# Coarse product, additions and tokens one step later in a software-pipelined attention, MoE and FFN kernel

## The chip, the cores and the metric

One core of a Trainium2 chip runs one program. The metric is device time in microseconds (us) of one execution, the median of several runs. Engines: PE (matrix products and transposes), DVE (vector), ACT (scalar), POOL (GpSimd), and the SP queue, which issues the DMA transfers. Each engine works through its own list in program order and waits by semaphores for the others.

## The reference, cut to what matters

```python
# attention: B=4, H=8, S=576, D=64; every part below feeds the next
q_d, k_d, v_d = (mean over groups of 4 rows of q, k, v)           # 144 coarse rows
out_up = repeat(softmax(q_d @ k_d.T / 8) @ v_d, 4)                # coarse attention
mask = |i - j| < 4
out_local = softmax(where(mask, q @ k.T / 8, -1e9)) @ v           # band of 7 keys
x = (out_up + out_local) as [2304, 512]                           # tokens
# soft MoE: 8 experts of 4 slots each
logits = x @ phi;  d = softmax over tokens;  slots = d.T @ x
slot_out[e] = relu(slots[e] @ w1[e]) @ w2[e]
x = softmax over slots(logits) @ slot_out
# FFN
out = relu(x @ w_in) ** 2 @ w_out
```

## The kernel before, in words

The attention is cut into 16 **units** (one batch and two heads each; four units make a batch). A unit passes through some twenty small steps, each a function that the program calls by a letter. The string `ORDER` lists these letters once; the loop `for s in range(3, NU)` calls the whole string in every **step** s, and gives each letter the unit that it works on: a letter of unit s-3 belongs to work begun three steps earlier. So one step touches units s to s-3, and the order in which each engine meets its instructions is the order of the letters. Nothing reorders them afterwards. `START` and `DRAIN` are lists written by hand for the filling and the emptying of the pipeline.

The letters, with the unit that they take in step s:

- `Q` loads q and k (unit s+2), `L` loads v (s-1), `l` loads a few weight pieces for the later stages.
- `T` (s): twelve PE transposes of q and k (tiles `tr`, L389), read out by ACT (`q`, L395) and by ACT and DVE (`kz`, L397). `d` (s): POOL sums groups of four rows into `qkd`.
- `S` (s-1): the local scores on PE (tile `s`), then on DVE the maximum `mx` (L427) and the subtraction into `elp` (L428). `E`: ACT's exponential of `elp` (L433).
- `s` (s-1): the coarse scores on PE (`sd`); `m`: their maximum on DVE (L447); `e`: three exponentials on ACT into `pd` (L454).
- `n`, `N` (s-1): sums and reciprocal on DVE, the scalings on POOL (`pl`, `pd`).
- `p` (s-2): transposes of the local probabilities (`ptp`), read out by ACT into `pt` (L482). `q` (s-2): transposes of the coarse probabilities (`pdp`), read out by ACT into `pdt` (L494).
- `V` (s-3): the local product on PE into two PSUM banks `av`, which carry sums of v along (L506). `x`: these sums are copied to `vt` (L516). `X`: two PE transposes of `vt` (`vdp`, L526), copied by DVE to `vd` (L527). `D`: the coarse product on PE from `vd` and `pdt` into the second bank `av` (L536), read out by ACT into `xd` (L541). `A`: DVE adds `av` and `xd` into the tokens `xt` (L549).
- `t` (s-3): the logits of the tokens (`lgt`, L567) and five transposes of `xt` (`xp`, `xrp`), read out by ACT (`xk`, `xr`). For the last unit of a batch `t` also runs the batch's softmax over tokens (`stage_g1`: a chain DVE, ACT, DVE), and one step later `g` and `G` transpose its result and form the batch's sums on PE (`stage_g2`, `stage_g3`, tile `sip`).
- `c`: DVE turns pieces of w_in from 64-bit to 32-bit words ("narrowing", L226 to L232): a turn of five phases, two instructions each. `CONV` says how many phases step s takes.

All transposes share one PSUM tag of three buffers (`bt`), so a transpose waits until the third one before it has been read out. `av` has two buffers, which are the two banks of one unit: `V` of the next unit waits until `A` has read them. `vt`, `vd`, `xd`, `xt`, `pt`, `elp`, `pl`, `pd`, `pdt` have one buffer each.

After the attention the experts and the FFN follow (from about 222 us to the end), which the change does not touch.

## Time and profile before

| | |
|---|---|
| time, median of 3 runs | 505.5 us (503.65 to 506.02) |
| the profiled execution's own time | 500.57 us |
| its span, first to last instruction | 498.9 us |
| busy share of the span | PE 89%, DVE 57%, ACT 54%, POOL 19% |
| mean granted clock of PE | 0.928 of full speed |
| weights, q, k and v read | 65.07 MB, 140 GB/s over the span |

The span holds stages with different limits: the attention to about 222 us, the experts to about 262 us, then the FFN. [...] A busy PE in the profile includes the modelled end of each product, so busy time is no measure of work when the clock is low.

### The profile page before, as it was taken

Reading aid. Unit: us, or ns where it says so; the run is one execution under the profiler, and the core shown is the slowest. Engines: PE = TensorE matmul, PEld = TensorE weight load, DVE = VectorE, ACT = ScalarE, POOL = GpSimd, SP = SyncE. Lnnn points to the kernel's source line nnn. Section 1 sums busy time; section 2 is a strip of 40 time slices with the busy share of each in tenths; the row PEclk is TensorE's granted clock in tenths of the full one; section 3 lists DMA queues with packets and bytes.
Section 4 is the critical chain, followed back from the end, with each engine's and each line's share of the span. In section 5 each row is a group of like instructions: output and inputs, shape, how many; then the busy total and the mean of one; then the engine's idle time right before and its main releaser. Section 6 shows DMA issues by size and latency. Waiting matters only on the chain.

```text
span 498.9 us, 10561 instructions
## 1 busy us (share of the span) xinstructions
PE 446.2 (89%) x4130; PEld 339.0 (68%) x4130; DVE 286.8 (57%) x624; ACT 267.6 (54%) x681; POOL 95.2 (19%) x169
## 2 busy tenths in 40 slices
PE   6687879788988778789998899999999999999996
PEld 5465656566666555554546678788888888888884
DVE  5655465645565566432408999994654645546452
ACT  5576555556454453322248889887544444444441
POOL 8255444444443333200200000000000000000000
PEclk9799878977787778899999999999999999999999
DMA  8966853854555534499999900000300100100101
GB/s 198 309 202 195 246 154 103 245 159 136 164 165 155 154 112 152 148 328 359 397 400 409 367 2 0 2 0 1 127 0 1 64 1 0 64 1 27 38 0 64
DMA packets 48875, 70.47 MB, mean 141 GB/s; under 512 B 23866, under 2 KB 30266, under 8 KB 48826
## 3 DMA queue, kind: packets, MB, share of 16 engines
q1 hardware_dynamic: 48682, 69.67, 42.7%
q8 instruction: 32, 0.52, 0.4%
q14 instruction: 17, 0.14, 0.1%
q10 hardware_dynamic: 144, 0.13, 0.1%
HBM read 65.07 MB, written 4.72 MB: 140 GB/s over the span
## 4 chain that ended last, share of the span: by engine, by line
PE 71%; DVE 15%; ACT 10%; issue 2%; DMA 1%; DVEq 0%; ACTq 0%
PE po L1029 36%; PE sd L443 4%; PE hp L837 3%; PE s L419 3%; PE ptp L481 3%; PE so L861 3%; PE up L969 3%; PE av L536 3%; ACT pd L454 3%; DVE kz L397 2%; PE pdp L493 2%; PE tr L389 2%; DVE win L231 2%; PE av L506 2%; ACT q L395 2%
## 5 line engine op out<-in xcount | busy, mean ns | idle before, releaser
L1029 PE MATMUL po<-wparts,ghi 128*128 128x512 f32 x576 | 149.1, 392 | 2.3 <-DVE wparts L927 2.3
L1029 PEld LDWEIGHTS po<-wparts,ghi 128*128 128x128 f32 x576 | 106.7, 188 | 23.8 <-DVE wparts L927 3.7
L974 ACT ACTIVATE r<-up 128x384 f32<-128x384 f32 x96 | 46.9, 489 | 72.8 <-PE up L969 68.6
L1029 PE MATMUL po<-wparts,glo 128*128 128x512 f32 x288 | 81.6, 391 | 0.5 <-DVE glo L982 0.5
L978 DVE TENSOR_TENSOR r<-r 128x384 f32<-128x384 f32 x64 | 35.6, 556 | 58.6 <-ACT ghi L977 58.6
L1029 PEld LDWEIGHTS po<-wparts,glo 128*128 128x128 f32 x288 | 53.9, 188 | 12.3 <-DVE glo L982 1.2
L982 DVE TENSOR_TENSOR glo<-r,ghi 128x384 fp32r<-128x384 f32 x94 | 52.3, 557 | 13.6 <-ACT ghi L981 7.5
L977 ACT ACTIVATE ghi<-r 128x384 fp32r<-128x384 f32 x66 | 34.7, 526 | 2.1
L969 PE MATMUL up<-cst,ast 128*128 128x384 f32 x96 | 33.0, 345 | 0.7 <-DVE ast L960 0.4
L395 ACT ACTIVATE q<-tr 64x288 f32<-64x288 f32 x64 | 27.2, 426 | 10.2 <-PE tr L389 9.4
L467 POOL TENSOR_TENSOR pl<-elp,sm 64x350 f32<-64x350 f32 x30 | 24.9, 831 | 26.3 <-DVE sm L465 11.5
L427 DVE TENSOR_REDUCE mx<-s 128x10 f32<-128x350 f32 x16 | 8.4, 522 | 33.3 <-PE s L419 33.2
L482 ACT COPY pt<-ptp 128x464 f32<-128x464 f32 (+1 forms) x32 | 11.3, 407 | 29.7 <-PE ptp L481 29.7
L407 POOL TENSOR_TENSOR qkd<-s 128x144 f32<-128x144 f32 x30 | 12.8, 425 | 74.0 <-PE sd L443 59.2
L506 PEld LDWEIGHTS av<-pt,vw 64*64 64x64 f32 x640 | 22.6, 139 | 3.5 <-issue 2.3
L506 PE MATMUL av<-pt,vw 64*64 64x73 f32 (+1 forms) x640 | 25.0, 232 | 0.0
L536 PE MATMUL av<-pdt,vd 72*64 72x144 f32 x128 | 15.0, 369 | 9.8 <-DVE vd L527 9.8
L389 PE MATMUL tr<-ident,k 96*128 96x96 f32 x96 | 15.2, 271 | 9.4 <-ACT q L395 9.0
L443 PE MATMUL sd<-qkd 64*64 64x144 f32 x192 | 22.6, 391 | 0.0
L397 DVE COPY kz<-tr 64x288 f32<-64x288 f32 x32 | 14.6, 458 | 12.4 <-PE tr L389 12.0
L541 ACT ACTIVATE xd<-av 128x288 f32<-128x288 f32 x16 | 6.6, 410 | 28.2 <-PE av L536 28.2
L969 PEld LDWEIGHTS up<-cst,ast 128*128 128x128 f32 x96 | 17.9, 188 | 5.2 <-DVE ast L960 0.7
(193 smaller groups left out, 729.7 us busy)
## 6 DMA issues: line engine op xcount, KB each, us to landing
w<-in_moe_w_dram SPq DMA_DIRECT2D x64, 512.0 KB, 6.4
win<-in_moe_w_in_dram SPq DMA_DIRECT2D x16, 512.0 KB, 7.7
wout<-in_moe_w_out_dram SPq DMA_DIRECT2D x16, 512.0 KB, 10.2
vw<-in_v_dram SPq DMA_DIRECT2D x30, 160.0 KB, 4.3
q<-in_q_dram SPq DMA_DIRECT2D x16, 288.0 KB, 3.2
k<-in_k_dram SPq DMA_DIRECT2D x16, 288.0 KB, 4.0
out_dram<-o SPq DMA_DIRECT2D x17, 256.0 KB, 2.3
vw<-in_v_dram SPq DMA_DIRECT2D x2, 144.0 KB, 5.6
```

Source lines behind the costliest of these rows:

```text
L389: nc.tensor.transpose(t[:, :, i], st[nm][:, h, 128 * i:128 * i + 128], ident[0:96, 0:96])
L395: nc.scalar.mul(out=o, in_=i_, mul=1.0 / 128.0)
L443: nc.tensor.matmul(sd[rr, t], qkd[rr, 0, 48 * t:48 * t + 64], qkd[rr, 1, 0:144], start=True, stop=True)
L467: (nc.vector if u in NDVE else nc.gpsimd).tensor_tensor(out=pl[r, :, c0:c0 + W], in0=el[r], in1=sm[r, 0:NB].unsqueeze(2).to_broadcast([64, ...
L506: nc.tensor.matmul(av[a][rr, VC * i:VC * i + n], vw[rr, 2 * i + a], pt[rr, i, a, 0:n], start=True, stop=True, tile_position=(64 * h, 64 * ...
L536: nc.tensor.matmul(dn[rr], st["vd"][:, a, rr], st["pdt"][:, a, :, h], start=(a == 0), stop=(a == 1), skip_group_check=True,)
L969: nc.tensor.matmul(t, ast[:, 128 * f:128 * f + 128], cst[:, c * n:c * n + n], start=True, stop=True)
L974: nc.scalar.activation(out=r, in_=t, func=AF.Relu)
L977: nc.scalar.activation(out=ghi, in_=r, func=AF.Square)
L978: nc.vector.tensor_tensor(out=g, in0=r, in1=r, op=ALU.mult)
L982: nc.vector.tensor_tensor(out=glo, in0=g, in1=ghi, op=ALU.subtract)
L1029: nc.tensor.matmul(po[c][i], a[:, 128 * i:128 * i + 128], w[f], start=(f == 0 and w is whi and a is ghi), stop=(f == NF - 1 and a is glo), ...
```

## The change

`T` now only transposes q; the keys get a letter of their own, `K`, which stands behind the scores `S` and `s`. `D` and `A`, and with them the tokens `t` (and `g`, `G` after them), move to the next step: they take unit s-4 and not s-3. `D` and `A` open the step. `pd` and `pdt` get two buffers, since the coarse probabilities now live one step longer. Both copies into `vt` go to DVE (the first was ACT's). `START` and `DRAIN` are written to match.

```diff
-ORDER = "VxTXQLgDSApsEdmqenGtNlc"
+ORDER = "DTAgSEsmKQdVxLepGtnXNqlc"
-START = "T0 Q2 d0 f10 T1 Q3 S0 s0 E0 d1 m0 T2 Q4 e0 f2 n0 l3 N0 S1 p0 s1 E1 q0 d2 m1 e1 n1 N1 l3"
+START = "T0 K0 Q2 d0 f10 T1 K1 Q3 S0 s0 E0 d1 m0 T2 K2 Q4 e0 f2 n0 l3 N0 S1 p0 s1 E1 q0 d2 m1 e1 n1 N1 l3"
-DRAIN = "V13 x13 L15 l3 p14 X13 D13 A13 S15 E15 s15 a m15 q14 e15 n15 N15 l c1 V14 x14 t13 X14 D14 A14 c1 p15 q15 V15 x15 X15 f1 D15 l c1 t14 A15 f6 t15 l"
+DRAIN = "D12 S15 A12 V13 x13 L15 l3 g2 E15 s15 a G2 t12 m15 p14 X13 q14 e15 n15 N15 l D13 c1 A13 V14 x14 t13 p15 X14 q15 D14 A14 V15 x15 c1 t14 X15 f1 D15 l c1 A15 f6 t15 l"
...
-        def transposes(u):
+        def transposes(u, js=(0,)):
             st = U[u]
-            for j, nm in enumerate("qk"):
+            for j in js:
+                nm = "qk"[j]
...
-            pd = ap.tile([128, 3, 144], F32, tag="pd", name=f"pd{u}")
+            pd = ap.tile([128, 3, 144], F32, tag="pd", bufs=2, name=f"pd{u}")
...
-            pdt = ap.tile([72, 2, 3, 2, 48], F32, tag="pdt", name=f"pdt{u}")
+            pdt = ap.tile([72, 2, 3, 2, 48], F32, tag="pdt", bufs=2, name=f"pdt{u}")
...
-            for a, c0, n, copy in ((0, 0, NC0, nc.scalar.copy), (1, NC0, NC1, nc.vector.tensor_copy)):
-                copy(
+            for a, c0, n in ((0, 0, NC0), (1, NC0, NC1)):
+                nc.vector.tensor_copy(
...
-                **dict.fromkeys("SEsmenN", u1), **dict.fromkeys("pq", u2), **dict.fromkeys("VxXDAt", u3),
+                **dict.fromkeys("SEsmenN", u1), **dict.fromkeys("pq", u2), **dict.fromkeys("VxX", u3), **dict.fromkeys("DAt", u4),
...
-                    if last(u4):
-                        (stage_g2 if x == "g" else stage_g3)(u4 // NP)
+                    if last(u5):
+                        (stage_g2 if x == "g" else stage_g3)(u5 // NP)
...
-                if x == "T" and s >= NU - 2:
+                if x == "K" and s >= NU - 2:
                     free.extend((ring, f"{y}{s % 2}") for y in "qk")
```

What this does on PE, at step 5 (the number behind a tile's name is its unit; for `ptp` and the others the first number). Before, from V(2) to p(3):

```order
L506 MATMUL av2_0_754<-pt_146,vw0_130 64x73 x10
L506 MATMUL av2_1_755<-pt_146,vw0_130 64x72 x10
L389 MATMUL tr5_00_779<-ident_67,q5_479 128x96 x3
L389 MATMUL tr5_01_785<-ident_67,q5_479 128x96 x3
L389 MATMUL tr5_10_791<-ident_67,k5_481 128x96 x3
L389 MATMUL tr5_11_797<-ident_67,k5_481 128x96 x3
L526 MATMUL vdp2_804<-ident_67,vt2_776 72x128 x2
L536 MATMUL av2_1_755<-pdt2_710,vd2_803 64x144 x4
L413 LDWEIGHTS identb_72
L413 MATMUL s4_819<-maskb_120,identb_72 128x350
L419 MATMUL s4_819<-kz0_139,q0_136 29x70 x20
L481 MATMUL ptp3_0_848<-ident_67,pl_165 128x128 x4
```

Now the step opens with D(1) and the transposes of q(5), and V(2) comes behind the scores and the keys:

```order
L390 MATMUL tr5_00_734<-ident_67,q5_484 128x96 x3
L390 MATMUL tr5_01_740<-ident_67,q5_484 128x96 x3
L414 LDWEIGHTS identb_72
L414 MATMUL s4_749<-maskb_120,identb_72 128x350
L420 MATMUL s4_749<-kz0_139,q0_136 29x70 x20
L444 MATMUL sd4_776<-qkd_161 64x144 x6
L390 MATMUL tr5_10_784<-ident_67,k5_486 128x96 x3
L390 MATMUL tr5_11_790<-ident_67,k5_486 128x96 x3
L507 MATMUL av2_0_807<-pt_146,vw0_130 64x73 x10
L507 MATMUL av2_1_808<-pt_146,vw0_130 64x72 x10
L482 MATMUL ptp3_0_838<-ident_67,pl_165 128x128 x4
L482 MATMUL ptp3_4_844<-ident_67,pl_165 128x128
```

In the first list X (`vdp`) follows the transposes and D follows X at once. In the second, D(1) opens the step (the row `av1_1<-pdt1,vd1`), S follows the transposes of q, and V(2) stands behind K. The end of the same step, from the transposes of the tokens on, holds the X(2) and D(2) of that V:

```order
L577 MATMUL xp1_855<-ident_67,xt1_746 128x128 x4
L580 MATMUL xrp1_861<-ident_67,xt1_746 64x128
L527 MATMUL vdp2_870<-ident_67,vt2_829 72x128 x2
L494 MATMUL pdp3_0_876<-ident_67,pd3_669 72x112 x3
L494 MATMUL pdp3_1_881<-ident_67,pd3_669 72x112 x3
L537 MATMUL av2_1_808<-pdt2_712,vd2_869 64x144 x4
```

X(2) is now followed by six transposes of `pd` before D(2) wants its result.

On DVE, around the narrowing of step 4 (`win`), the rows before:

```order
L465 RECIPROCAL sm3_679<-sm3_679 128x13
L229 TENSOR_SCALAR win0_0_588<-win0_0_588 128x512 x2
L516 COPY vt2_776<-av2_1_755 128x5x14
L397 COPY kz1_144<-tr5_11_797 64x288 x2
L527 COPY vd2_803<-vdp2_804 72x256
L427 TENSOR_REDUCE mx4_841<-s4_819 128x10
L428 TENSOR_TENSOR elp_163<-s4_819,mx4_841 128x10x35
L549 TENSOR_TENSOR xt2_845<-av2_0_754,xd_159 128x5x58
L549 TENSOR_TENSOR xt2_845<-av2_1_755,xd_159 128x5x58
```

and the rows now:

```order
L465 TENSOR_SCALAR sm3_607<-sd3_611 128x3
L466 RECIPROCAL sm3_607<-sm3_607 128x13
L528 COPY vd1_706<-vdp1_707 72x256
L229 TENSOR_SCALAR win0_0_561<-win0_0_561 128x512 x2
L550 TENSOR_TENSOR xt1_746<-av1_0_642,xd_159 128x5x58
L550 TENSOR_TENSOR xt1_746<-av1_1_643,xd_159 128x5x58
L428 TENSOR_REDUCE mx4_771<-s4_749 128x10
L429 TENSOR_TENSOR elp_163<-s4_749,mx4_771 128x10x35
L448 TENSOR_REDUCE mx4_771<-sd4_776 128x3
```

Before, the additions (`xt`) stood behind `mx` and `elp` of the scores, and the copies of the next unit right behind the narrowing. Now the additions of unit 1 stand between the narrowing and `mx4`, and both copies to `vt` are DVE's. The SP queue issues the same transfers in the same order as before, and the number of PE instructions is the same.

## Rows read from the trace of the kernel before

**Rows 1.** Stretches: length; busy of PE, PEld, DVE, ACT, POOL (instructions); PEclk; DMA share; GB/s.

```profile
40.13:49.96 9.83, 8.34 (x150) 6.47 (x148) 5.81 (x14) 6.76 (x21) 5.32 (x8) 1.00 0.71 203
...
60.30:74.66 14.36, 11.54 (x151) 8.75 (x150) 7.75 (x19) 7.74 (x26) 6.02 (x8) 0.74 0.60 161
...
30.32:181.57 151.25, 125.13 (x1792) 93.45 (x1791) 86.80 (x193) 84.64 (x269) 67.45 (x97) 0.83 0.59 171
...
181.57:222.08 40.51, 33.90 (x431) 24.00 (x429) 20.42 (x52) 14.08 (x48) 8.33 (x12) 0.87 0.53 184
```

**Rows 2.** Timeline of one step: start us, duration us, engine, line, instruction [idle before it].

```profile
41.83 0.70 ACT L482 COPY pt<-ptp 128x464 f32<-128x464 f32 x2 [1.17 <-PE ptp L481]
...
41.90 0.52 DVE L428 TENSOR_TENSOR elp<-s,mx 128x350 f32<-128x350 f32 x1
...
42.33 0.82 DVE L549 TENSOR_TENSOR xt<-av,xd 128x290 f32<-128x290 f32 x2
...
42.45 0.49 ACT L433 ACTIVATE elp<-elp 128x350 f32<-128x350 f32 x1
...
42.71 0.80 PE L493 MATMUL pdp<-ident,pd 112*72 112x112 f32 x6
...
43.85 0.39 ACT L454 ACTIVATE pd<-sd,mx 128x144 f32<-128x144 f32 x1
...
44.54 1.48 PE L506 MATMUL av<-pt,vw 64*64 64x73 f32 x40
...
45.08 0.16 ACT L454 ACTIVATION_READ_ACCUMULATOR pd<-sd,mx 128x1 f32 x1
...
45.13 0.63 ACT L577 COPY xk<-xp 128x512 f32<-128x512 f32 x1
...
45.65 0.25 ACT L580 COPY xr<-xrp 64x128 f32<-64x128 f32 x1
...
45.95 0.71 PE L389 MATMUL tr<-ident,q 96*128 96x96 f32 x6
...
46.50 0.41 PE L389 MATMUL tr<-ident,k 96*128 96x96 f32 x3
...
47.37 0.47 PE L389 MATMUL tr<-ident,k 96*128 96x96 f32 x3 [0.46 <-ACT q L395]
...
48.23 0.85 ACT L397 COPY kz<-tr 64x288 f32<-64x288 f32 x2
...
48.26 0.44 PE L526 MATMUL vdp<-ident,vt 128*72 128x128 f32 x2 [0.42 <-ACT q L395]
...
49.31 0.71 PE L536 MATMUL av<-pdt,vd 72*64 72x144 f32 x8 [0.61 <-DVE vd L527]
```

**Rows 3.** Busy time by stretch, two stretches of 2 us.

```profile
46.00:48.00 2.00, 1.38 (x14) 1.01 (x12) 1.18 (x3) 1.52 (x5) 1.85 (x3) 1.00 0.19 52
...
58.00:60.00 2.00, 1.30 (x10) 0.98 (x10) 1.04 (x3) 0.85 (x3) 0.98 (x2) 0.74 0.78 217
```

**Rows 4.** Timeline of PE: the first of a batch's two sums (stage_g3).

```profile
80.03 1.07 PE L635 MATMUL sip<-xk,ee 128*32 128x512 f32 x8
```

**Rows 5.** Timeline of DVE: the first and a late link of a batch's softmax.

```profile
119.37 0.25 DVE L600 TENSOR_REDUCE mb<-lgt 128x1 f32<-128x144 f32 x1
...
121.30 0.92 DVE L613 SCALAR_TENSOR_TENSOR srun<-srun,al,sb 128x1 f32<-128x1 f32 x1
```

**Rows 6.** DVE by line and shape, 30 to 200 us: count | busy, mean ns | idle.

```profile
L231 DVE SCALAR_TENSOR_TENSOR win<-win,win 128x512 int32<-128x512 int32 x6 | 7.1, 1225 | 0.0
...
L229 DVE TENSOR_SCALAR win<-win 128x512 f32<-128x512 f32 x8 | 6.8, 894 | 0.0
...
L226 DVE TENSOR_SCALAR win<-win 128x512 int32<-128x512 int32 x8 | 5.4, 719 | 0.0
...
L232 DVE SCALAR_TENSOR_TENSOR win<-win,win 128x512 int32<-128x512 int32 x6 | 5.4, 941 | 0.0
...
L230 DVE TENSOR_SCALAR win<-win 128x512 int32<-128x512 int32 x8 | 4.6, 617 | 0.0
```

## The prediction

> **What bounds the kernel now.** I read first the busy times by stretch, cut at the starts of the units' local scores S, then the timeline of one step, and then the clock. From S(2) at 30.32 to S(14) at 181.57 the kernel takes 151.25 us for 12 steps. PE is busy in 125.13 of them and idle in 26.1, at a mean clock of 0.83; DVE is busy 86.8, ACT 84.6, the DMA engines 0.59 of the time [rows 1]. So PE bounds this part by a mixture of waits and low clock, and no other engine is full. A step at full clock, from S(3) to S(4), takes 9.83 us, of which PE works 8.34 [rows 1]. The missing 1.49 us are three waits, and the bracket behind the row says for what [rows 2]: the second pair of key transposes waits 0.46 for ACT's copies of q (they hold the buffer), X waits 0.42 for the same copies, and D waits 0.61 for DVE's copy `vd` of X's result. All three stand in one stretch, between V and the next S.

> This stretch also costs clock. From 46 to 48 us PE worked 1.38 of 2.00 us and the clock stayed at its upper level. Around 58 to 60 us it worked 1.30 of 2.00, and the clock fell to the lower level within that stretch [rows 3]. The step from S(6) to S(7), which begins behind that fall and sees another, has a mean clock of 0.74 and takes 14.36 us, with 2.82 idle [rows 1]. Against 9.83 with 1.49 idle, the low clock costs 14.36 - 9.83 - (2.82 - 1.49) = 3.2 us in that step.

> **The change, part by part.** I walk one step of the new order at full clock.

> *The waits removed.* The keys now stand behind S and s, so ACT has long finished q; X stands behind t and is followed by six transposes before D. These three waits, 1.49 us a step, lose their causes. What could take their place is the circle through ACT and DVE. From the rows of the step [rows 2]: S to the end of `elp` is 41.90 + 0.52 - 40.13 = 2.29; then E 0.49, the keys' copies on ACT 0.85, the three exponentials e from 43.85 to 45.24 = 1.39, `pt` 0.70, `xk` and `xr` from 45.13 to 45.90 = 0.77; the last transposes of `pd` wait for that buffer, about half of their 0.80, 0.40; D 0.65 (49.31 to S at 49.96); the transposes of q 0.55 (45.95 to 46.50); and S again. The sum is 8.09, with some 0.03 for each of eight handings-over 8.35. PE's own work is 8.34. So the new step is 8.35 us: both bounds lie together, and there is no slack on ACT for more.

> *The start.* S(2) no longer stands behind V(0), the keys, X and D. In the shown step V starts at 44.54, and S 5.42 later [rows 2]; less 0.55 for q this is 4.9, so S(2) comes at about 25.3. The first step then still fills the pipeline; I give it no price.

> *Twelve steps.* 12 x 8.35 = 100. Two batches form their sums in them, two parts of about 1.07 us each [rows 4] with two transposes ahead, 5 together. Those transposes hold the bank of the coarse scores until ACT has read them, two copies in which I see 0.5 a batch, an estimate from the size of `xr`: 1.

> *The batch's softmax.* Its DVE links used to stand at the step's end. Now they stand ahead of the sums n, the reciprocal and `vd`. The chain from `mb` at 119.37 to the end of `srun` at 122.22 takes 2.85 us and waits on ACT inside [rows 5], and D waits behind `vd`. I take 2.4 of it on the path, twice: 4.8. Bounds: nothing, if the six transposes cover it, and 5.7.

> *The narrowing.* It stands on DVE right behind `vd` and now ahead of `xt` and `mx`, as the rows of the order show; behind a late `xt` wait V on PE and `mx`, `elp` on DVE, and behind these E and all that follows it on ACT. From the end of `vd` to the time when `mx` can start there are D 0.65, q 0.55 and S 1.15 (the 2.29 above less `mx` and `elp`, 0.52 and about as much, and their gaps), and `vd` ends some 0.15 ahead of D. Less 0.85 for `xt` (0.82 [rows 2] and a gap) this leaves room for about 1.65 us. The phases take two instructions each: 1.4 (L226), 1.8 (L229), 1.2 (L230), 2.45 (L231), 1.9 (L232) [rows 6]. By CONV the steps 6, 8, 11, 12 and 13 have 2.45, 3.2, 4.35, 3.2 and 3.7 us, over the room by 0.8, 1.6, 2.7, 1.6 and 2.0; two steps with L229 or L232 alone add 0.2 each. That makes 9. Step 12's own sums on PE hide most of the 2.7, so I take 7. Below, nothing, if DVE gets ahead in other steps; above, 9. The second copy to `vt`, 0.2 us more on DVE, is hidden by PE's V behind which it stands.

> *The clock.* With 1.49 us of idle gone from each step, the clock should stay up except where the narrowing or a batch's softmax tears a hole of over 1.5 us: some four or five of the steps. A fall costs up to 3.2 us (above); I take 4 falls at 2.5, 10 us. Bounds: none, 0, and one in every step, 38.

> Together S(14) comes at 25.3 + 100 + 5 + 1 + 4.8 + 7 + 10 = 153 and not 181.6.

> *The end.* From S(14) to the experts it takes 40.51 us now, with PE busy 33.90 [rows 1]. D, A and t come a step later, so behind S(14) stand in addition the keys of 15, V, t, X and D of an earlier unit: 2.5 (one V and t lie between the end of `pdp` and the transposes of q, 43.45 to 45.95) + 0.55 + 0.4 + 0.65 = 4.1 [rows 2]. And two new waits: three phases of narrowing (1.4 + 1.8 + 1.2 = 4.4 [rows 6]) now stand ahead of A(12), for which V(13) waits; and L231, behind the reciprocal of unit 15, stands ahead of A(13), for which V(14) waits. Walked through, these leave PE idle about 4 us each. Some waits of the old end go. I take 4.1 + 7.4 = 11.5 more, 52 in all; bounds 46 and 55.

> *What it is hidden by.* The expert stage streams weights. The SP queue issues the same loads in the same steps, so what lies in store at the experts' start is the same, and the stage only moves. The DMA engines are busy 0.59 of 12.6 us, 7.4 us a step [rows 1]; in a step of 10.6 that still fits, and q and k are loaded two steps ahead.

> *The sum.* The attention ends at 153 + 52 = 205 against 222: 17 us less. The profiled execution took 500.6 (its span of 498.9 and 1.7 around it), so the changed one would take 483.8. The runs shown lie 3 to 5.5 above the profiled one; I add 3.4 and predict 487 us for the median, against 505.5.

> [...] Behind p the new order has, at full clock, some four us in which PE does little but transposes: p, the tokens, X, `pd` and q, with two short products between. In the stretch from 46 to 48 us PE did transposes for most of its 1.38 us, idled for 0.62, and the clock stayed up [rows 3], so transposes seem to hold it. [...]

> **The rivals.**
> 1. *The clock hardly falls at all.* The holes of 2 us are too short or lie apart, as in the step from 40.13, where 1.49 us did not bring it down [rows 1]. Then 10 us less: 477; with the narrowing partly hidden 470.
> 2. *The clock falls in every step, and the kernel gets slower.* The mechanism: the long stretch of transposes and short products with every small wait in it lets the clock fall once a step. Price: 3.2 us in each of 12 steps, 38 in place of 10, and 2 in the end: 487 + 30 = 517. Without any fall the change gains 17 + 10 = 27, so it decides from 27 / 3.2, about nine falls in 12 steps, on. For it: the old stretch did bring falls. Against it: those had 1.49 us and more of idle in them.
> 3. *DVE becomes the bound.* DVE's queue is in order, and narrowing, additions and maxima are now one chain. If the room is 0.5 less than I think, all phases in 11 steps overrun: about 5 more, and the end's waits cost 5 more: 497. For it: DVE works 7.2 us a step already. Against: in steps of few phases it idles over 2 us.
> 4. *The change moves waits but not the time.* The end gives back all that the steps gain: this needs falls at the full price in most steps or loads that come late; 500 to 508.

> **How the numbers follow.** My forecast (478 to 495) has a chance of 0.50, rival 1 0.18, rival 3 0.18, rival 2 0.08, rival 4 0.06. The low end is rival 1 with most narrowing hidden and the short end, 468; the high end is rival 3 with two or three falls more, 504; this leaves out the slow rivals and the best case. A change of 0.5%, 2.5 us, is about what a measurement of this kernel can tell from none. Faster: 0.50 + 0.18 + 0.18 and a little of rival 4, 0.87; within 0.5%, most of rival 4, 0.04; slower, rival 2 and a little, 0.09.

> **What the profile of the changed kernel would show.** Steps without narrowing at full clock of 8.3 to 8.7 us from S to S; no wait of the key transposes for ACT's q, none of X for `vt`, and D waiting for `vd` only behind a batch's softmax; V waiting for `xt` where two phases of narrowing stand ahead; PE's mean clock above 0.9 between S(2) and S(14), which lasts 120 to 135 us; the end some 52 us. The prediction is wrong if the clock falls in most steps, if ACT's circle is longer than 9 us, if PE waits for loads of q, k or v, or if the end costs 60.

## The result and the profile after

The changed kernel takes 470.97 us (469.12 to 475.89, 4 runs) against 505.01 (503.65 to 506.02, 4 runs) for the kernel before on the same chip: a ratio of 0.9343, 95% interval 0.9268 to 0.9417. It is faster by 34 us, nearly twice the forecast's gain, and near the low end of its range, 468 to 504. (Ratios here leave disturbed executions out, so they can differ a little from the ratio of two medians.) The profiled execution took 470.79 us, 29.8 less than that of before.

The busy times of the stretches that answer to [rows 1]: one quiet step, one with a batch's softmax, S(2) to S(14), and the end up to the experts. Columns as there.

```profile
44.46:52.80 8.34, 8.11 (x149) 6.43 (x148) 5.71 (x15) 6.84 (x21) 5.93 (x9) 1.00 0.82 247
61.14:73.03 11.89, 9.34 (x152) 7.41 (x150) 7.64 (x22) 8.04 (x25) 6.42 (x9) 0.91 0.87 242
26.34:138.87 112.53, 102.53 (x1769) 78.89 (x1767) 75.63 (x201) 84.56 (x256) 77.52 (x98) 0.98 0.76 220
138.87:192.18 53.31, 40.98 (x511) 29.85 (x508) 23.15 (x68) 17.50 (x59) 11.95 (x15) 0.79 0.50 167
```

PEclk is the granted clock, as a mean over the stretch. Cut into stretches of 1 us, the first 490 us of the kernel before show 1.00 in 404 of them, 0.50 in 60 (from 59 to 65 us, for one) and values between in 26; 1.00 and 0.50 are the upper and the lower level meant here.

The gain lies in the twelve steps, 112.5 us where there were 151.3, at a clock of 0.98 where it was 0.83, and in the start: S(2) comes 4.0 us earlier. The end gives 12.8 us back (53.3 against 40.5), at 0.79 where it was 0.87. The stage behind it only moves: from the first expert product to the end of the span it takes 276.76 us, before 276.78. Seven of the twelve steps take 8.34 us each. The four that hold a batch's softmax or its sums take 11.89, 11.08, 9.88 and 11.50, and the first takes 9.77.

The timeline of PE in the quiet step (start, duration, instruction, idle before it) shows the new order, to be set beside [rows 2].

```profile
46.33 0.71 PE L390 MATMUL tr<-ident,k 96*128 96x96 f32 x6
...
50.23 0.44 PE L527 MATMUL vdp<-ident,vt 128*72 128x128 f32 x2
...
50.91 0.77 PE L494 MATMUL pdp<-ident,pd 112*72 112x112 f32 x6 [0.23 <-ACT xr L581]
...
51.61 0.71 PE L537 MATMUL av<-pdt,vd 72*64 72x144 f32 x8
```

The waits of the keys (0.46), of X (0.42) and of D (0.61) are gone; one of 0.23 us, for ACT's `xr`, is what is left. PE's waits from 15 to 215 us, by what ended them (total, times, longest):

```profile
PE av L507 <- DVE xt L550: 7.4, 3, 3.7
PE av L537 <- DVE vd L528: 4.0, 4, 1.3
PE pdp L494 <- ACT xr L581: 3.4, 12, 0.4
...
PE ptp L482 <- issue: 1.0, 1, 1.0
```

The first row is the end: V of units 13, 14 and 15 waits for `xt`. The second is D: three times behind a batch's softmax, as foreseen, 1.1 to 1.3 us each, and once 0.4 in the end. The last names no other engine; it comes back below.

DVE's narrowing, by line, from 25 to 200 us (count, busy, mean ns), to be set beside [rows 6]:

```profile
L231 DVE SCALAR_TENSOR_TENSOR win<-win,win 128x512 int32<-128x512 int32 x8 | 5.6, 745 | 0.0
L232 DVE SCALAR_TENSOR_TENSOR win<-win,win 128x512 int32<-128x512 int32 x8 | 5.1, 680 | 0.0
...
L229 DVE TENSOR_SCALAR win<-win 128x512 f32<-128x512 f32 x8 | 3.0, 416 | 0.0
L230 DVE TENSOR_SCALAR win<-win 128x512 int32<-128x512 int32 x8 | 3.0, 416 | 0.0
L226 DVE TENSOR_SCALAR win<-win 128x512 int32<-128x512 int32 x8 | 3.0, 412 | 0.0
```

Every phase became shorter, from 1225, 941, 894, 617 and 719 ns. What became longer is POOL's scaling into `pl`, first after, then before, in the same stretch:

```profile
L468 POOL TENSOR_TENSOR pl<-elp,sm 64x350 f32<-64x350 f32 x30 | 38.7, 1291 | 37.9 <-DVE sm L466 36.8
```

```profile
L467 POOL TENSOR_TENSOR pl<-elp,sm 64x350 f32<-64x350 f32 x28 | 22.8, 815 | 16.5 <-DVE vt L516 7.8 <-ACT xk L577 5.9 <-DVE sm L465 1.8
```

In the steps `pl` is needed only one step later, so its 476 ns more an instruction cost nothing there.

### The profile page after: what moved, and what is told of

The parts are those of the page before. It is cut to its first block, busy times and chain, and to the rows that moved or that the text cites. A ratio compares the mean times of both kernels' runs of the same rounds, so it can differ in the third digit from the quotient of the medians.

```text
span 468.9 us, 10607 instructions
## 1 busy us (share of the span) xinstructions
PE 428.2 (91%) x4130; PEld 328.4 (70%) x4130; DVE 276.0 (59%) x640; ACT 267.0 (57%) x665; POOL 106.2 (23%) x169
## 4 chain that ended last, share of the span: by engine, by line
PE 69%; ACT 15%; DVE 9%; issue 3%; DMA 2%; POOL 1%; DVEq 0%; ACTq 0%; POOLq 0%
PE po L1032 38%; PE hp L840 4%; ACT pd L455 4%; PE so L864 3%; PE up L972 3%; PE tr L390 3%; PE av L507 3%; PE s L420 2%; DMA q<-in_q_dram 2%; PE pdp L494 2%; PE av L537 2%; ACT kz L398 2%; ACT pt L483 2%; ACT xk L578 2%; PE sd L444 1%
## 5 line engine op out<-in xcount | busy, mean ns | idle before, releaser
L468 POOL TENSOR_TENSOR pl<-elp,sm 64x350 f32<-64x350 f32 x30 | 38.7, 1291 | 37.9 <-DVE sm L466 36.8
L507 PE MATMUL av<-pt,vw 64*64 64x73 f32 (+1 forms) x640 | 27.2, 244 | 7.4 <-DVE xt L550 7.4
L507 PEld LDWEIGHTS av<-pt,vw 64*64 64x64 f32 x640 | 24.7, 149 | 9.6 <-DVE xt L550 8.2
L406 POOL TENSOR_TENSOR s<-kz 64x288 f32<-64x288 f32 x30 | 19.8, 661 | 10.5 <-ACT kz L398 9.1
L578 ACT COPY xk<-xp 128x512 f32<-128x512 f32 x16 | 9.4, 585 | 22.0 <-PE xp L577 22.0
L972 PEld LDWEIGHTS up<-cst,ast 128*128 128x128 f32 x96 | 17.9, 188 | 5.2 <-ACT r L977 0.7
L550 DVE TENSOR_TENSOR xt<-av,xd 128x290 f32<-128x290 f32 x32 | 13.2, 453 | 11.4 <-ACT xd L542 11.4
L455 ACT ACTIVATE pd<-sd,mx 128x144 f32<-128x144 f32 x48 | 18.3, 381 | 2.0 <-DVE mx L448 0.6
L444 PE MATMUL sd<-qkd 64*64 64x144 f32 x192 | 16.7, 311 | 2.6 <-ACT etr L629 1.7
L390 PE MATMUL tr<-ident,q 96*128 96x96 f32 x96 | 13.2, 283 | 6.1 <-DMA q<-in_q_dram 6.1
L840 PE MATMUL hp<-w,sT 128*32 128x256 f32 x256 | 17.7, 428 | 0.4 <-DVE sT L787 0.4
```

What stands on the lines that cost most here:

```text
L390: nc.tensor.transpose(t[:, :, i], st[nm][:, h, 128 * i:128 * i + 128], ident[0:96, 0:96])
L455: nc.scalar.activation(out=pd[:, t], in_=sd[:, t], func=AF.Exp, bias=mx[:, 10 + t:11 + t], accum_out=ss[:, t:t + 1],)
L468: (nc.vector if u in NDVE else nc.gpsimd).tensor_tensor(out=pl[r, :, c0:c0 + W], in0=el[r], in1=sm[r, 0:NB].unsqueeze(2).to_broadcast([64, ...
L507: nc.tensor.matmul(av[a][rr, VC * i:VC * i + n], vw[rr, 2 * i + a], pt[rr, i, a, 0:n], start=True, stop=True, tile_position=(64 * h, 64 * ...
L840: nc.tensor.matmul(t[32 * g:32 * g + 32], sT[:, kt], got["w1", e, kt][:, 256 * g:256 * g + 256], start=(kt == 0), stop=(kt == 3), tile_pos ...
L972: nc.tensor.matmul(t, ast[:, 128 * f:128 * f + 128], cst[:, c * n:c * n + n], start=True, stop=True)
```

## The experiments

My theory after the result: the gain has two parts, the waits (12 x 1.49 = 17.9 us) and the clock, which no longer falls because these waits were what made it fall. The rival: the clock has another cause, or the waits would have moved elsewhere without one of the two shifts (keys, and D with its followers).

**The clock alone: the kernel before, its three waits filled.** Small products stand in the waits of [rows 2], so that the order of PE's other work stays as it was and PE is busy while it waits.

```diff
+                    if j and h and u >= 3:
+                        busy(4)
                     t = bt([128, 96, 3], f"tr{u}_{j}{h}")
...
+            busy(4)
             t = bt([72, 2, 128], f"vdp{u}")
...
             dn = st["av"][1][:, VC * NB // 2:VC * NB // 2 + 144]
+            busy(5)
```

> The kernel before, with its three PE waits of each step filled by small products on the identity (4 ahead of the last key transposes, 4 ahead of X, 5 ahead of D, as the warm-up products are); nothing waits less. Theory, that idle time in the stretch between V and S brings the clock down and that half of the change's gain is clock: mean granted clock from S(2) to S(14) from 0.83 to above 0.93, steps without narrowing stay at about 9.8 us, some 15 to 20 us gained over 12 steps, about 487 us. Rival, that the clock has nothing to do with the waits or that the gain is the waits alone: clock as before, time 503 to 512.

Measured: 479.31 us (478.23 to 479.7, 4 runs), ratio 0.9521 [0.9457, 0.9586]. S(2) to S(14) and the end:

```profile
31.63:163.21 131.58, 121.46 (x1949) 92.08 (x1947) 86.06 (x193) 84.96 (x269) 67.57 (x97) 1.00 0.70 196
163.21:202.56 39.35, 35.25 (x457) 25.36 (x456) 20.28 (x52) 14.02 (x48) 8.35 (x12) 0.91 0.57 192
```

With 157 instructions more on PE, the same twelve steps take 19.7 us less, and the clock is 1.00 where it was 0.83. The kernel gains more than the 15 to 20 us expected. The clock alone was worth about 20 us there, which is shown. The other part is what remains: from here to the changed kernel it is 19.1 us (131.6 to 112.5), near the 17.9 of the waits.

**The keys alone moved** (the kernel before, `K` behind `s`, `p` and `E`, and with it the loads `Q`; D, A and t where they were).

```diff
-ORDER = "VxTXQLgDSApsEdmqenGtNlc"
+ORDER = "VxTXLgDSApsEKQdmqenGtNlc"
```

> The kernel before with one part of the change: the key transposes stand behind the local and the coarse scores; D, A and t stay in their step. Theory: the wait of the keys for ACT's q goes (0.46 a step), X waits for the copies to vt and D for vd as before or longer, so steps at full clock of about 9.2 to 9.4 and a clock that still falls: 488 to 500 us. Rival, that the keys' place is the main part: below 480.

Measured: 501.04 us (498.5 to 501.72, 10 runs), ratio 1.0015 [0.9978, 1.0051]: nothing, so it lies in neither of the two ranges expected. PE's waits, 30 to 180 us:

```profile
PE vdp L527 <- DVE vt L517: 20.3, 8, 3.5
PE av L537 <- DVE vd L528: 5.5, 12, 0.5
PE pdp L494 <- ACT kz L398: 4.5, 12, 0.4
```

The waits only moved: X now waits up to 3.5 us for `vt`, which stands behind the narrowing, and D and the coarse transposes wait in all twelve steps. The clock is 0.89 from S(2) to S(14), and S(2) to S(14) takes 150.8.

**D, A and t alone moved** (the changed kernel, `K` right behind `T` as before).

```diff
-ORDER = "DTAgSEsmKQdVxLepGtnXNqlc"
+ORDER = "DTKAgSEsmQdVxLepGtnXNqlc"
```

> The changed kernel with one part undone: the keys are transposed right behind the queries again; D, A and t stay a step later. Theory: the last keys wait about 0.6 us for ACT's q, X and D wait for nothing, so steps of about 8.9 in place of 8.34, the clock stays up: about 478 us. Rival, that the keys' place carries the gain: 490 and more.

Measured: 481.07 us (480.63 to 481.95, 4 runs), ratio 0.9562 [0.9498, 0.9626]. PE's waits up to S(14):

```profile
PE tr L390 <- ACT q L396: 6.6, 12, 1.8
PE xrp L580 <- ACT pt L483: 6.3, 9, 0.7
```

The wait of the keys for ACT's q stays, and a new one for `pt` comes, which I had not expected; a quiet step takes 9.38 us, not 8.9. So the shift of D carries most of the gain, some 20 us, and the keys' shift, worth nothing alone, is worth some 10 with it.

**The idle time given back** (the changed kernel with nine small memsets on DVE ahead of the copy `vd`, so that D waits).

```diff
+            for _ in range(9):
+                nc.vector.memset(junk, 0.0)
             nc.vector.tensor_copy(vd, t)
```

> The changed kernel with nine DVE fills of a small unused tile ahead of the copy vd, about 2.5 us of DVE work a unit, so that D waits about 1.5 us in each step: as much idle time as the old step had, in the new order. Theory, that idle time brings the clock down: steps of 9.9 at full clock, and in several of them a fall at 2 to 3 us more; mean clock from S(2) to S(14) below 0.90; 500 to 515 us. Rival, that the new order keeps the clock whatever PE waits: 12 x 1.5 and some 4 in the end more, about 493 us, with a clock as in the changed kernel.

Measured: 524.84 us (520.91 to 527.55, 4 runs), ratio 1.0422 [1.032, 1.0524], slower than the kernel before and beyond the 500 to 515 expected. S(2) to S(14), and D's waits in it:

```profile
25.91:183.73 157.82, 121.15 (x1769) 93.07 (x1768) 104.66 (x311) 84.98 (x256) 65.74 (x99) 0.83 0.55 163
```

```profile
PE av L540 <- DVE vd L531: 29.9, 12, 4.7
```

D waits 2.5 us a step on average, and the clock is at 0.83 again, in the new order with its long run of transposes. The 45.3 us that the steps lose are more than D's waits, 29.9 in all: at the lower clock PE's own work grows too, its busy time from 102.53 to 121.15 us. So the clock follows PE's idle time in one order as in the other. The memsets also delay the rest of DVE's queue, so this does not give the price of a single wait.

**The copy to `vt` on ACT again.** The first of the two copies goes back to `nc.scalar.copy`.

> The changed kernel with one part undone: the first copy to vt is ACT's again, 0.23 us more on ACT in a step. Theory, that ACT's circle is as long as PE's work: quiet steps of 8.5 to 8.6 in place of 8.34, two to three us in all, 473 to 474. Rival, that ACT has room: quiet steps of 8.34, 471.

Measured: 471.13 us (470.58 to 477.24, 6 runs), ratio 0.9438 [0.9374, 0.9501]. Quiet steps take 8.37 to 8.38 us, 0.03 more; S(2) to S(14) 113.0 against 112.5. ACT had room for it.

**One buffer of `pdt`.** `pdt` loses its second buffer.

> The changed kernel with one buffer of pdt, so that ACT's copies of the coarse probabilities wait for D of the unit before. Theory, that ACT has only the wait for E as room: xd and the copies of q come 0.7 us later, quiet steps of 8.4 to 8.8, 472 to 477. Rival, that the second buffer is needed at every step: over 9 us a step, 480 and more.

Measured: 475.83 us (474.19 to 479.14, 4 runs), ratio 0.9514 [0.9447, 0.9581]. Quiet steps take 8.66 us, so the buffer is worth 0.32 a step, about 4 us in twelve. S(2) to S(14) is 121.9; the rest of its 9.4 us more came with a stall of 2.6 us (below) and a clock of 0.94, in the slowest of the four executions. The second buffer of `pd` wasn't tried alone.

**The narrowing right behind x** (before the copies of the sums n and of `vd`, near its old place).

```diff
-ORDER = "DTAgSEsmKQdVxLepGtnXNqlc"
+ORDER = "DTAgSEsmKQdVxcLepGtnXNql"
```

> The changed kernel with the narrowing ahead of the sums n and of vd, where POOL is at work on its key sums, and not behind vd. Theory, that the narrowing cost nothing because it found POOL not yet at work and so took 0.41 to 0.75 us an instruction, not 0.62 to 1.2: here 0.6 to 1.0 again, D waits for vd in every step with narrowing, steps with two phases 2 us longer, clock falls there: 482 to 490 us. Rival, that its place does not matter: 471.

Measured: 477.89 us (475.89 to 478.46, 4 runs), ratio 0.954 [0.9481, 0.9598]. Its L226 and POOL's `pl`, as above, and D's waits up to S(14):

```profile
L226 DVE TENSOR_SCALAR win<-win 128x512 int32<-128x512 int32 x8 | 5.7, 757 | 0.0
```

```profile
L468 POOL TENSOR_TENSOR pl<-elp,sm 64x350 f32<-64x350 f32 x30 | 23.7, 792 | 46.3 <-DVE sm L466 43.2 <-PE pdp L494 1.9
```

```profile
PE av L537 <- DVE vd L528: 5.0, 3, 3.0
```

With the place, the two durations change back: L226 from 412 to 757 ns, `pl` from 1291 to 792. D waits three times, up to 3.0 us, and not in each step with narrowing: quiet steps with one phase take 8.34 to 8.41 us. The time lies below the 482 to 490 expected. So it is the place on DVE that makes the narrowing short. The expectation's reason, that POOL is not yet at work there, was wrong: `pl` is at work, and it is the one that takes longer. Here it is in a quiet step of the changed kernel, with the narrowing beside it:

```profile
51.01 1.43 POOL L468 TENSOR_TENSOR pl<-elp,sm 64x350 f32<-64x350 f32 x1
```

```profile
51.05 0.75 DVE L230 TENSOR_SCALAR win<-win 128x512 int32<-128x512 int32 x2
```

Of the 30 `pl` of the changed kernel from 25 to 200 us, the 14 that overlap a narrowing take 1886 ns on average, the 16 others 770. So in this kernel `pl` is the one that takes longer beside a narrowing, although by the recorded starts, which are rough on POOL, it comes 0.04 us ahead of the narrowing in the step above. What holds it up is not shown.

**The end in another order** (no narrowing in step 15; `c5` behind `x13`, D(13) and A(13) ahead of `e15`).

```diff
-... V13 x13 L15 ... q14 e15 n15 N15 l D13 c1 A13 V14 ...
+... V13 x13 c5 L15 ... q14 D13 A13 e15 n15 N15 l V14 ...
```

> The changed kernel with another end: the three phases of narrowing of step 15 and two of the drain's single ones stand together behind the copies to vt of unit 13, where DVE idled for almost six us, and D and A of unit 13 stand ahead of e and n of unit 15. Theory, that narrowing ahead of the additions makes V(13) and V(14) wait 2.7 and 3.7 us and brings the clock down there: the end from S(14) to the experts 46 to 48 us in place of 53.3, 463 to 466 us. Rival, that the end is long for its added work and its chain of dependent steps: 52 to 53 and about 470.

Measured: 470.26 us, with a spread of 460.19 to 477.83 over six runs (ratio 0.9244 [0.9144, 0.9344]). PE's waits for `xt` fall from 7.4 to 3.7 us, yet the profiled execution, the slowest of the six, has an end of 54.6 us at a clock of 0.70. Over the six the time goes with the mean clock, 0.932 at 477.83 and 0.985 at 460.19. In the profiled one S(2) to S(14) takes 117.8 us, 5.3 more than in the changed kernel, with a stall of 3.2 us (below) in it. It left open what the order is worth.

**The changed kernel with small products in the remaining waits.** `F` is a run of small products in a buffer of the transposes.

```diff
             dn = st["av"][1][:, VC * NB // 2:VC * NB // 2 + 144]
+            if u in (3, 7, 11):
+                busy(10)
-DRAIN = "D12 S15 A12 V13 ... G2 ... c1 A13 V14 ... A14 V15 ..."
+DRAIN = "D12 S15 A12 F18 V13 ... F4 G2 ... c1 A13 F26 V14 ... A14 F8 V15 ..."
```

> The changed kernel with small products in the places where TensorE still stands: 10 ahead of D of units 3, 7 and 11 (each waits 1.1 to 1.25 us there), 18 ahead of the values of unit 13, 26 ahead of those of unit 14, 8 ahead of those of unit 15 (they wait 2.7, 3.7 and 1.05 us) and 4 ahead of the first sip. Nothing else is changed. Theory that the end (53.3 us at a granted clock of 0.79) is long because the clock falls behind its waits: it keeps a clock of 0.95 or more, takes 46 to 48 us, and the kernel 462 to 466 us. Rival that the end's length is set by VectorE's narrowing and what follows it, whatever the clock: it stays at 52 to 54 us and the kernel at 470 to 472 us.

Measured: 469.34 us (465.4 to 471.83, 6 runs), ratio 0.9388 [0.9315, 0.9461].

```profile
25.09:143.87 118.78, 108.65 (x1799) 83.95 (x1798) 76.30 (x202) 84.72 (x256) 78.96 (x99) 0.96 0.72 212
143.87:192.07 48.20, 42.10 (x565) 30.45 (x563) 23.11 (x68) 17.44 (x59) 10.98 (x14) 0.96 0.54 178
```

The end did as the theory says, 53.3 to 48.2 at 0.96, but the kernel missed the 462 to 466 expected. The steps lost it again, in part since I had the wrong units: the D that waits is that of units 4, 8 and 12. Ahead of 3, 7 and 11 nothing waited, and the ten products lengthened three steps from 8.34 to 9.44. The rest is two falls of the clock in this execution.

**Both: the other order of the end, and the small products** (F8, F12 and F8 ahead of V13, V14 and V15, F4 ahead of G2, the same `busy(10)`).

> The end in the other order of the experiment on it (no narrowing in the last step, D(13) and A(13) earlier), with small products where it still waits: 8 ahead of the values of unit 13, 12 ahead of those of unit 14, 8 ahead of unit 15, 4 ahead of the first sip, and 10 ahead of D of units 3, 7 and 11. That order alone gave 460 to 478 us, the longer the lower its mean clock (0.985 to 0.932). Theory that the clock is what spreads it: the runs lie together at 458 to 463 us with a mean clock above 0.98. Rival that the clock falls for another cause than these waits: the spread stays above 8 us.

Measured: 465.21 us (463.56 to 468.51, 6 runs), ratio 0.9326 [0.9265, 0.9387].

```profile
25.73:140.52 114.79, 104.37 (x1799) 80.59 (x1797) 75.70 (x201) 84.80 (x256) 78.68 (x99) 1.00 0.77 221
140.52:184.84 44.32, 37.72 (x542) 26.87 (x540) 22.71 (x68) 17.73 (x59) 8.38 (x14) 0.98 0.62 201
```

The time misses the 458 to 463 expected by 2.2 us; the ten products ahead of the wrong D cost 3.3. The spread shrank from 17.6 to 5.0 us and the end takes 44.3, so the clock behind the waits was in the main what spread the former. The stall, 3.2 us in the former's slowest execution and 0.5 here, is a part of the spread that the filling does not explain.

**The same with the products ahead of the right D** (units 4, 8, 12, `busy(8)`).

> The kernel of the experiment on the other order of the end with small products, with the ones ahead of D moved to the units whose D does wait (4, 8 and 12; before they stood ahead of D of units 3, 7 and 11, where nothing waited and they lengthened three steps from 8.34 to 9.44 us), and 8 of them instead of 10. Theory: these 3.3 us come back, S(2) to S(14) takes 111 to 112 us at a clock of 1.00 and the kernel 460 to 463 us. Rival that the step's length there is set by VectorE's chain behind the batch's softmax and not by the order of TensorE: the time stays at 464 to 466 us.

Measured: 463.85 us (460.0 to 465.33, 6 runs), ratio 0.9328 [0.9237, 0.9418]. S(2) to S(14), the end, and a stretch near the start:

```profile
26.66:141.69 115.03, 105.89 (x1785) 81.74 (x1783) 75.70 (x201) 84.88 (x256) 77.76 (x98) 0.97 0.74 216
141.69:186.01 44.32, 38.63 (x550) 27.64 (x547) 22.72 (x68) 17.71 (x59) 9.39 (x15) 0.98 0.63 207
34.45:41.27 6.82, 6.72 (x73) 5.08 (x73) 2.75 (x7) 3.26 (x9) 3.85 (x5) 0.50 0.68 210
```

The three steps are back at 8.34 to 8.35 us. In the profiled execution a fall of the clock in the first and second step took the 3.0 us away again (11.31 and 9.84 us where the run above had 9.78 and 8.34), so the 111 us of the theory are not shown, and the time falls between its 460 to 463 and the rival's 464 to 466. All six runs lie below the lowest of the changed kernel (469.12), though those were measured at another time, and the intervals of the two ratios overlap.

**Twelve small products ahead of the step of S(4)** ask what the wait named "issue" is.

```diff
-FILL = {0: 8, 1: 16, 2: 10, 3: 0, 16: 5, ...
+FILL = {0: 8, 1: 16, 2: 10, 3: 0, 5: 12, 16: 5, ...
```

> The changed kernel with 12 small products more ahead of the step that issues S(4), about 1.3 us of TensorE's work, and nothing else. It asks what the stall of 0.8 to 3.2 us without a releaser is, which the changed order shows at the second ptp transpose of the step from S(6) to S(7), always the matmul of the same number in the program. Theory that it belongs to a place in the stream of instructions: it moves 12 products earlier, into the values ahead of those transposes (vw and pt). Rival that it belongs to that operation or to what the queues carry at that time: it stays at the ptp transposes. In either case the kernel takes 471 to 474 us.

Measured: 472.12 us (469.83 to 478.49, 4 runs), ratio 0.9444 [0.9359, 0.9528]. PE's timeline at the wait, in the changed kernel and in this one:

```profile
65.07 0.33 PE L482 MATMUL ptp<-ident,pl 128*128 128x128 f32 x1
66.39 0.60 PE L482 MATMUL ptp<-ident,pl 128*128 128x128 f32 x4 [0.99 <-issue]
```

```profile
66.33 0.98 PE L507 MATMUL av<-pt,vw 64*64 64x73 f32 x24
68.83 0.59 PE L507 MATMUL av<-pt,vw 64*64 64x72 f32 x10 [1.52 <-issue]
```

It moved from the second `ptp` to a product of V eleven earlier: it belongs to a place in PE's stream of instructions, not to the operation.

## Why the prediction was right, and where its terms were off

- **The whole.** The time lies in the range, but below my forecast of 478 to 495. What came is rival 1: a clock that hardly falls, and a narrowing that is hidden.
- **The step.** 8.35 us predicted, 8.34 measured, in seven of twelve steps. The working had one error: "there is no slack on ACT for more". ACT took a copy of `vt` back for 0.03 us a step. Of the two bounds that I set equal, PE's was the one that held. That it agrees to 0.01 us is luck: I had PE at 8.34 us of work without a wait, and it has 8.11 and a wait of 0.23.
- **The start.** S(2) at 26.34, 25.3 predicted (my own terms give 25.4); and the first step, which I gave no price, cost 9.77 - 8.34 = 1.4.
- **The batch's softmax and sums.** 4.8 + 6 = 10.8 predicted; the four steps take 44.35 - 4 x 8.34 = 11.0 more. The second batch, with neither stall nor fall, shows the terms: 1.54 us for the softmax (2.4 predicted) and 3.16 for the sums (3.0). Twice that is 9.4, so the terms were 1.4 too high. The first batch's 1.6 on top are the stall without a releaser, 1.0, and the one fall of the clock, about 0.6. The fall was cheap here because most of it was hidden. These are the same two steps, first in the changed kernel, then in the run with both the other end and the small products, where the clock did not fall:

```profile
61.14:73.03 11.89, 9.34 (x152) 7.41 (x150) 7.64 (x22) 8.04 (x25) 6.42 (x9) 0.91 0.87 242
73.03:84.11 11.08, 10.58 (x158) 7.28 (x157) 5.99 (x16) 6.53 (x22) 5.92 (x8) 0.94 0.61 168
```

```profile
61.63:72.09 10.46, 8.41 (x151) 6.72 (x150) 7.03 (x21) 7.65 (x24) 4.51 (x7) 1.00 0.75 207
72.09:83.58 11.49, 10.02 (x159) 6.91 (x157) 6.69 (x18) 7.09 (x23) 6.85 (x9) 1.00 0.72 209
```

  Less their stalls (1.0 and 0.5) the pairs take 22.0 and 21.45 us. In the second step PE waits 1.0 us at the coarse scores for ACT's copy `etr` at the full clock, and not at all behind the fall.
- **The narrowing, 7 us, was mis-sized: it cost 0.** No step without a softmax or sums is longer for it. I priced its phases by [rows 6]; at their new place they take 412 to 745 ns, so one phase, 0.8 to 1.4 us, fits the room of 1.65 us that I had worked out. The room was too small as well: from S(12) to S(13) two phases take 2.19, and the maximum behind them still waits for PE's scores.

```profile
129.46 1.28 DVE L231 SCALAR_TENSOR_TENSOR win<-win,win 128x512 int32<-128x512 int32 x2
130.66 0.81 DVE L550 TENSOR_TENSOR xt<-av,xd 128x290 f32<-128x290 f32 x2
131.65 0.52 DVE L428 TENSOR_REDUCE mx<-s 128x10 f32<-128x350 f32 x1 [0.18 <-PE s L420]
```

  A duration measured at one place on DVE was carried to another. The experiment that puts the narrowing elsewhere shows that.
- **The clock, four falls and 10 us, was mis-sized: one fall in the profiled execution, about 0.6.** The mechanism was right, as the filled waits show on the kernel before (0.83 to 1.00 from S(2) to S(14)) and the returned idle time on the changed one (0.98 to 0.83). What I overrated were the holes: the narrowing made none, and D's waits were only 1.1 to 1.3 us. The one fall came in the step that holds both the stall and a wait of D. That these brought it down is not shown: with stalls of 1.39 and 1.52 us and the same wait of D in that step, two other runs (the copy to `vt` on ACT, the twelve products) show no fall there: D's products take 0.71 us in both, 1.02 in the changed kernel. Where no wait hid it a fall cost more: with the products ahead of the right D, the one in the first and second step took 3.0 us.
- **The end.** 52 predicted, 53.3 measured, by the two waits named: V(13) waits 2.7 us behind three phases and then behind POOL's `pl`, for which `elp` waits on DVE; V(14) 3.7, of which L231 takes 1.80, behind the reciprocal of unit 15. The agreement is partly luck. PE idles 5.7 us more than before, where I had 7.4, and is busy 7.1 more, where I had 4.1, as the clock there fell from 0.87 to 0.79. I had given the clock of the end no price; filled, at 0.96, the end took 48.2. DVE's timeline at the first wait:

```profile
147.21 0.75 DVE L226 TENSOR_SCALAR win<-win 128x512 int32<-128x512 int32 x2
...
150.80 0.52 DVE L429 TENSOR_TENSOR elp<-s,mx 128x350 f32<-128x350 f32 x1 [1.08 <-POOL pl L468]
151.24 0.82 DVE L550 TENSOR_TENSOR xt<-av,xd 128x290 f32<-128x290 f32 x2
```

  Here the longer `pl`, free in the steps, is paid for.
- **The sum.** The attention's end came at 192.2 and not 205: 14.1 us earlier at S(14) (7 of narrowing, 9.4 of clock and 1.4 of softmax and sums, less 1.0 of the stall, 1.0 and 1.4 of the start and 0.3 of rounding) and 1.3 later by the end. The 3.4 us that I added from profile to median were wrong as well, 0.2 here. So it came nearest to rival 1 (470 to 477).
- **A reading.** The step of 14.36 us, 60.30 to 74.66, which I called the one from S(6) to S(7), is that from S(5) to S(6). No number changes by it.
- **The stretch of transposes.** The 517 us of rival 2 did not come. A stretch of the quiet step in which PE does only transposes, and the steps around it:

```profile
49.48:51.61 2.13, 1.90 (x26) 1.34 (x14) 1.30 (x5) 1.62 (x7) 1.98 (x4) 1.00 0.69 155
26.51:70.89 44.38, 38.78 (x705) 30.62 (x705) 28.86 (x80) 34.85 (x106) 29.85 (x41) 1.00 0.86 238
```

  The clock stayed at 1.00 through the three quiet steps from 36.1 to 61.1 us, each with such a stretch. Other products stand before and behind each stretch, so this shows only that 2.1 us of transposes between them did not bring the clock down, and not what transposes alone would do to it. No run here shows a longer stretch of them.

## What to carry to other kernels

Ask two prices of a wait, its length and what it costs through the clock, and tell them apart by filling the wait with small products: here 1.49 us of waits a step cost 17.9 us themselves and 20 more through the clock. A shift can be worth nothing alone and some 10 us beside another (here the keys beside D), when alone it leaves another wait standing; undo shifts one at a time before you call one useless. And carry a duration to a new place only after asking what ran beside it.

## What the runs showed of the hardware

The wait of PE without a releaser was not expected. Nine profiles have it, all of kernels in the new order, 0.2 to 3.2 us long, at the matmul of the same number in PE's stream (839th or 840th); one of them has a second, of 0.3 us, at the 2085th. The page lists a DMA queue of a kind of its own:

```profile
q8 instruction: 33, 0.54, 0.5%
```
